# First products of the token and channel mixing in two steps, and one DVE stretch for a head's output

## The chip, the cores and the metric

The kernel runs as one program on one core of a Trainium2 chip. The metric is the device time of one execution in microseconds (us). Five engines work side by side: TensorE (PE, with its weight loads shown apart as PEld), VectorE (DVE), ScalarE (ACT), GpSimd (POOL), and SyncE (SP), whose queue issues the DMA transfers. Each engine takes its own instructions in program order and waits for others by semaphores.

## What is computed

The reference chains three blocks, for a batch of 4, 8 heads, 576 positions and 64 numbers per head. Everything is float32 at the ends.

```
scores = q k^T / sqrt(D) + (cum_i - cum_j), causal        # cum = running sum of log f
attn   = exp(scores - max);  attn /= sum(attn) + 1e-9
x      = attn v                                            # [4, 576, 512]
h      = relu(x^T w_tok1) w_tok2                           # token mixing, over the positions
u      = x + h^T
y      = u + relu(u w_ch1) w_ch2                           # channel mixing, 512 -> 1536 -> 512
out    = (g * sigmoid(g)) w_out,  g = conv3(relu(y w_in))  # gated block, 512 -> 1024 -> 512
```

## The kernel before

**Splitting.** Products of the mixing blocks are made in float16 with each operand as a pair, a high part h and a low part l = value - h. One product of two pairs takes three matmuls, wh·xh, wh·xl and wl·xh. The helper `mm3` (lines 277 to 282) issues them in this order, and lines 280, 281 and 282 in the profile are these three, whoever called it.

**Loops.** There are 32 heads (batch times 8). Scores are made for pairs of heads (`score`), then `smax` (DVE) takes the row maximum, `sexp` (ACT) the exponential, and the result is transposed: by PE for the first 8 heads and the last (`ptr`), by a DMA for the others, which first splits it on POOL and DVE (`hi_part`, `lo_part`; the lines 1027 and 1033, tiles `ph` and `pl`). `pv` multiplies it with the values and, in a 65th column, sums it. `norm` (DVE) makes the reciprocal of the sum, and `xout` (DVE) writes the scaled x of the head, tile `xf`. `x_hi` (ACT) and `x_lo` (POOL) split it into `xh` and `xl`.

Four heads are a group (8 groups, two to a batch). For a group `t1` multiplies with w_tok1 (two calls with `a` = 0, 1; each 5 terms, 15 matmuls of 128x256), and `t2` with w_tok2, four times, onto a transpose of x. `u_copy` takes u to SBUF. Once both groups of a batch are there, `u_largest` (DVE, line 266, tile `um`), `u_span` (PE, line 260) and `u_scale` (DVE, tile `su`) find a power of two for the batch, and `u_part` splits u into `uh` (ACT) and `ul` (DVE, line 594), two halves of 288 positions, of which each comes in two steps.

`channel_mix` works on such a half: `m1` multiplies with a block of w_ch1 (per block four calls, `k` = 0 to 3, each three matmuls of 128x288), `rh` and `rl` apply the ReLU and split, `m2` multiplies with w_ch2. Of 12 blocks, 5 are done while the attention runs; the rest and the gated block come after it.

**What sets the order.** Every step is written down as a task with its engine, an estimated duration, a rank, the keys it reads and writes, and the PSUM ring it takes (`z`: 2 double banks, `w`: 4 banks). The planner `Order.run` simulates the engines with these estimates, takes at each point the open task that can begin first (ties by rank), and the instructions are written in that order. So a change to a task, a key or a rank moves instructions everywhere in the first half of the program. The constants that set the ranks are `TOKR`, `TOKP`, `VRANK`, `SETR`, `LATER` and `PER`.

In a task of `t1` all of `xh` and `xl` of the four heads are read; every task of `m1` reads all eight parts of u (`ukeys`: four of `uh`, four of `ul`).

## Time and profile before

| | us |
|---|---|
| median of 3 executions | 717.89 (717.03 to 718.03) |
| span of the profiled execution | 718.1 |
| PE busy | 698.7 (97% of the span), 6417 matmuls |
| PE weight loads | 561.1 (78%) |
| DVE busy | 507.4 (71%) |
| ACT busy | 428.5 (60%) |
| POOL busy | 243.4 (34%) |
| chain that ended last: on PE, on DVE | 87%, 8% |

The profiled execution is known by its span, which is within 0.1 us of the slowest of the three that were timed. The span can be read in two halves. Up to about 315 us attention, token mixing and the early channel mixing run interleaved; from there to the end PE works through the late channel mixing and the gated block. [...]

### The profile page before, as it was taken

How to read it: one execution, taken by the hardware profiler on the slowest of the kernel's cores; microseconds unless marked ns; L12 is line 12 of the kernel's file. 1: busy time of each engine (PE TensorE's matmuls, PEld its weight loads, DVE VectorE, ACT ScalarE, POOL GpSimd, SP SyncE). 2: the span in 40 equal slices, each digit the busy share in tenths (PEclk: the TensorE clock that was granted, in tenths of full speed). 3: DMA queues.
4: the chain of work that ended last, by engine and by line, in shares of the span. 5: the costliest groups of instructions: out<-in, count | busy, mean ns of one | idle time of the engine just before them, and what ended most of it. 6: DMA issues, size and time to landing. Idle time of an engine off the chain costs nothing.

```text
span 718.1 us, 16399 instructions
## 1 busy us (share of the span) xinstructions
PE 698.7 (97%) x6417; PEld 561.1 (78%) x6417; DVE 507.4 (71%) x1268; ACT 428.5 (60%) x940; POOL 243.4 (34%) x321
## 2 busy tenths in 40 slices
PE   6999888999999999999999999999999999999998
PEld 5889665878877788888888778778888778778786
DVE  6787878999987779537566857435778866875570
ACT  6987776586666544646574645112177766776671
POOL 2247562748453666240000212103023322322240
PEclk9999887999999999999999999999999999999999
DMA  9445769799995979785455765344211111100101
GB/s 225 141 127 189 193 175 235 120 258 226 248 239 138 199 122 223 189 282 150 144 172 147 250 221 161 99 133 144 66 56 58 51 59 34 51 27 25 34 17 50
DMA packets 153117, 101.98 MB, mean 142 GB/s; under 512 B 90000, under 2 KB 145168, under 8 KB 153040
## 3 DMA queue, kind: packets, MB, share of 16 engines
q1 hardware_dynamic: 152944, 100.79, 54.4%
q8 instruction: 50, 0.82, 0.5%
q14 instruction: 27, 0.22, 0.1%
q10 hardware_dynamic: 96, 0.15, 0.1%
HBM read 57.73 MB, written 23.59 MB: 113 GB/s over the span
## 4 chain that ended last, share of the span: by engine, by line
PE 87%; DVE 8%; ACT 1%; DMA 1%; SPq 1%; issue 1%; POOL 0%; DVEq 0%; ACTq 0%
PE w L280 15%; PE w L281 15%; PE w L282 15%; PE z L281 8%; PE z L282 8%; PE z L280 8%; PE z L994 6%; PE w L1083 3%; DVE pl L1033 2%; PE w L1051 2%; PE w L1235 2%; PE z L998 1%; PE w L260 1%; DVE ul L594 1%; PE w L1088 1%; PE w L1089 1%
## 5 line engine op out<-in xcount | busy, mean ns | idle before, releaser
L282 PEld LDWEIGHTS <-w 128*128 128x128 f16 x1280 | 125.6, 98 | 34.0 <-issue 1.9
L280 PEld LDWEIGHTS <-w 128*128 128x128 f16 x1280 | 125.3, 98 | 33.7 <-issue 2.4
L281 PEld LDWEIGHTS <-w 128*128 128x128 f16 x1280 | 125.3, 98 | 33.0 <-issue 1.7
L281 PE MATMUL w<-ul,w 128*128 128x288 f16 x416 | 120.0, 288 | 1.6 <-DVE ul L594 1.6
L280 PE MATMUL w<-uh,w 128*128 128x288 f16 x416 | 120.0, 289 | 1.3 <-ACT uh L591 1.1
L282 PE MATMUL w<-uh,w 128*128 128x288 f16 x416 | 119.9, 288 | 0.0
L275 POOL TENSOR_TENSOR g<-sg,g 128x286 f16<-128x286 f32 (+1 forms) x64 | 55.1, 867 | 150.8 <-ACT g L269 148.0
L1518 DVE SCALAR_TENSOR_TENSOR cv<-hp,cw,cv 128x286 f32<-128x286 f32 (+1 forms) x128 | 75.0, 593 | 38.3 <-ACT cv L1512 36.0
L1018 ACT ACTIVATE t<-t,m 128x192 f32<-128x192 f32 (+4 forms) x160 | 82.0, 551 | 18.1 <-DVE m L1012 14.9
L643 ACT ACTIVATE r<-w 128x288 f16<-128x288 f32 x96 | 39.3, 409 | 88.0 <-PE w L282 87.1
L1012 DVE CUSTOM_DVE_ANT_0 t<-z,mask 128x192 f32<-128x192 f32 (+4 forms) x160 | 70.3, 479 | 12.8 <-PE z L998 12.5
L720 POOL TENSOR_TENSOR p<-p,u 128x288 f32<-128x288 f32 x32 | 26.6, 863 | 149.7 <-DMA p<-p_d 115.1
L647 DVE SCALAR_TENSOR_TENSOR r<-w,r 128x288 f16<-128x288 f32 x96 | 43.3, 453 | 46.8 <-ACT r L643 46.2
L281 PE MATMUL z<-g,w 128*128 128x286 f16 (+1 forms) x256 | 73.3, 286 | 0.0
L280 PE MATMUL z<-g,w 128*128 128x286 f16 (+1 forms) x256 | 73.0, 285 | 0.0
L282 PE MATMUL z<-g,w 128*128 128x286 f16 (+1 forms) x256 | 72.9, 285 | 0.0
L280 PE MATMUL w<-vh,w 128*128 128x288 f16 x224 | 64.1, 286 | 0.0
L281 PE MATMUL w<-vl,w 128*128 128x288 f16 x224 | 64.1, 286 | 0.0
L282 PE MATMUL w<-vh,w 128*128 128x288 f16 x224 | 64.1, 286 | 0.0
L280 PE MATMUL z<-r,w 128*128 128x288 f16 x224 | 64.1, 286 | 0.0
L281 PE MATMUL z<-r,w 128*128 128x288 f16 x224 | 64.1, 286 | 0.0
L282 PE MATMUL z<-r,w 128*128 128x288 f16 x224 | 64.1, 286 | 0.0
(201 smaller groups left out, 1686.8 us busy)
## 6 DMA issues: line engine op xcount, KB each, us to landing
wraw<-in_moe_w_ch_dram SPq DMA_DIRECT2D x24, 512.0 KB, 4.2
qk<-in_qk_dram SPq DMA_DIRECT2D x15, 608.0 KB, 5.4
u_d<-us SPq DMA_DIRECT2D x8, 576.0 KB, 3.4
p_d<-res SPq DMA_DIRECT2D x32, 144.0 KB, 3.1
p<-p_d SPq DMA_DIRECT2D x8, 576.0 KB, 5.3
u<-u_d SPq DMA_DIRECT2D x8, 576.0 KB, 4.8
x_d<-p SPq DMA_DIRECT2D x8, 576.0 KB, 3.2
u<-x_d SPq DMA_DIRECT2D x8, 576.0 KB, 3.9
```

What stands on the lines that cost most here:

```text
L275: nc.gpsimd.tensor_tensor(o, a, b, ALU.subtract)
L280: nc.tensor.matmul(ps, wh, xh, start=(first and i == 0), stop=False)
L281: nc.tensor.matmul(ps, wh, xl, start=False, stop=False)
L282: nc.tensor.matmul(ps, wl, xh, start=False, stop=(last and i == n - 1))
L643: nc.scalar.activation(out=t[:, 0, :], in_=box["z", m], func=AF.Relu)
L647: nc.vector.scalar_tensor_tensor(t[:, 1, :], box["z", m], 0.0, f32(t[:, 0, :]), ALU.max, ALU.subtract)
L720: nc.gpsimd.tensor_tensor(box["p"][:, d], box["p"][:, d], box["u"][:, d], ALU.add)
L994: nc.tensor.matmul(out_[x], t[r, Q0[i]:Q0[i] + 128], t[r, k0:k0 + n], start=first, stop=False)
L1012: nc.vector.tensor_tensor_reduce(to, z_t.pop((n, i)), mk, -0.125, 3e38, ALU.add, ALU.min, m_t[n][0:rows, i:i + 1])
L1018: nc.scalar.activation(out=tt[0:rows, o:o + w], in_=tt[0:rows, o:o + w], func=AF.Exp, bias=m_t[n][0:rows, i:i + 1], scale=-1.0)
L1083: nc.tensor.matmul(o[:, 0:65], p32(n)[:, 128 * blk:128 * blk + 128], vp32_t[g % 2][:, slot, hh, :], start=(j == 0), stop=(j == nb - 1))
L1518: nc.vector.scalar_tensor_tensor(cv, hp_t[m][:, s0 + t:s1 + t], cw[:, t, m:m + 1], cv, ALU.mult, ALU.add)
```

## The change

`mm3` stays for the second products. For `t1` and `m1` two helpers take its place. `mm_high` issues the two matmuls with a high x (wh·xh, wl·xh), `mm_low` the one with a low x (wh·xl). `t1` becomes two tasks for each `a`: 10 matmuls that read `xh` only, then 5 that read `xl`. `m1` becomes five tasks for each block: four of 2 matmuls, `k` = 0 to 3, that each read only their own part of `uh`, and a fifth (`k` = 4) of 4 matmuls that reads all of `ul`. The number of matmuls is the same.

`norm` and `xout` become one task of three DVE instructions. The keys of `opening` are widened: the first writer of a half of u now claims all its parts.

The constants of the ranks change, and with them the order of the whole first half. The planner's durations are split with the tasks (`t1` 1.66 into 1.11 and 0.55, `m1` into MM * 2 and MM * KD).

```diff
-    TOKR, TOKP = 4.0, 5.0
-    VRANK = 10.0
-    SETR = ((-15.0, 20.0),)
-    LATER = (-60.0, 0.0, 20.0)
-    PER = 7.0
+    TOKR, TOKP = 4.32, 4.98
+    VRANK = 19.68
+    SETR = ((-10.9, 9.83),)
+    LATER = (-62.89, 79.29, 41.56)
+    PER = 7.03
...
+    def mm_high(ps, terms, first=True):
+        for i, (wh, wl, xh) in enumerate(terms):
+            nc.tensor.matmul(ps, wh, xh, start=(first and i == 0), stop=False)
+            nc.tensor.matmul(ps, wl, xh, start=False, stop=False)
+
+    def mm_low(ps, terms, last=True):
+        for i, (wh, xl) in enumerate(terms):
+            nc.tensor.matmul(ps, wh, xl, start=False, stop=(last and i == len(terms) - 1))
...
-        return {"reads": [("first", r - 1)], "writes": [("first", r)]}
+        return {"reads": [("first", r - 1)], "writes": [("first", r)] + [x for k in range(KD) for x in split_keys(r, k)]}
...
             wh, wl = halves("ch1", m)
+            if k == KD:
+                mm_low(box["z", m], [(wh[:, x, :], ul[:, x, :]) for x in range(KD)])
+                return
             if k == 0:
                 box["z", m] = flat_bank(tag)[:, 0:CH]
-            mm3(box["z", m], [(wh[:, k, :], wl[:, k, :], uh[:, k, :], ul[:, k, :])], k == 0, k == KD - 1)
+            mm_high(box["z", m], [(wh[:, k, :], wl[:, k, :], uh[:, k, :])], k == 0)
...
             for j in range(KD):
-                T("PE", MM * 3, rank + pe, m1, m, j, reads=[*ukeys, wkey("ch1", m)],
+                T("PE", MM * 2, rank + pe, m1, m, j, reads=[uhigh[j], wkey("ch1", m)],
                   writes=[kz, kr, (*kr, "l")], ring=[kz])
+            T("PE", MM * KD, rank + pe, m1, m, KD, reads=ulow, writes=[kz], ring=[kz])
...
             nc.vector.reciprocal(rs, rs)
-            rs_t[n] = rs
-
-        def xout(n):
             g, hh = divmod(n, HG)
...
-            o, rs = pv_t.pop(n), rs_t.pop(n)
+            o = pv_t.pop(n)
             nc.vector.tensor_tensor(x_of(n), o[:, :, 0:64], rs.unsqueeze(2).to_broadcast([128, NS, D]), ALU.mult)
...
-                T("DVE", 0.5, rank + 6, norm, n, reads=[kw, ("vsc", g % 3)], writes=[("rs", n % 2)], pools=A1, ring=[kw])
-                T("DVE", 0.46, rank + 6, xout, n, reads=[kw, ("rs", n % 2)], writes=[("xf", g % 2, n % HG)], pools=A1, ring=[kw])
+                T("DVE", 0.98, rank + 6, norm, n, reads=[kw, ("vsc", g % 3)], writes=[("xf", g % 2, n % HG)], pools=A1, ring=[kw])
...
-        def t1(g, a):
+        def t1(g, a, low):
             st = tok[g]
+            c = slice(a * 128, (a + 1) * 128)
+            if low:
+                mm_low(st["ps1", a], [(w1h[:, j, c], st["xl"][:, j, :]) for j in range(NS)])
+                return
             st["ps1", a] = bank("w")[:, 0:HG * D]
-            c = slice(a * 128, (a + 1) * 128)
-            terms = []
-            for j in range(NS):
-                terms.append((w1h[:, j, c], w1l[:, j, c], st["xh"][:, j, :], st["xl"][:, j, :]))
-            mm3(st["ps1", a], terms)
+            mm_high(st["ps1", a], [(w1h[:, j, c], w1l[:, j, c], st["xh"][:, j, :]) for j in range(NS)])
...
-                T("PE", 1.66, t0 + 3, t1, g, a, reads=[*xk, *W1K], pools=A1, ring=[kw],
+                T("PE", 1.11, t0 + 3, t1, g, a, False, reads=[*xk["xh"], *W1K], pools=A1, ring=[kw],
                   writes=[kw, ("t1h", a), ("t1l", a)])
+                T("PE", 0.55, t0 + 3, t1, g, a, True, reads=xk["xl"], pools=A1, ring=[kw], writes=[kw])
```

Three places show what the new order does.

The first is on DVE, at the last head of group 1 (head 7), whose x the group's `t1` needs. `um<-us` is `u_largest` of group 0, `rs` and `xf` are the sum's reciprocal and x of head 7, `pl` the low split of heads 8 (t_194) and 9 (t_195). Before:

```order
L266 TENSOR_REDUCE um_87<-us 128x1
L555 SCALAR_TENSOR_TENSOR w_123<-w_113,pw_c_238,w_123 128x512
L1033 SCALAR_TENSOR_TENSOR pl<-t_194,ph 128x640
L1095 TENSOR_SCALAR rs<-w,vsc 128x5
L1098 RECIPROCAL rs<-rs 128x5
L1033 SCALAR_TENSOR_TENSOR pl<-t_195,ph 128x1024
L1106 TENSOR_TENSOR xf<-w,rs 128x5x64
```

Now:

```order
L1045 SCALAR_TENSOR_TENSOR pl<-t_195,ph 128x1024
L1045 SCALAR_TENSOR_TENSOR pl<-t_195,ph 128x640
L266 TENSOR_REDUCE um_87<-us 128x1
L330 TENSOR_SCALAR wraw<-wraw 128x512
L331 SCALAR_TENSOR_TENSOR w_118<-w_118,wraw 128x512
L1107 TENSOR_SCALAR rs<-w,vsc 128x5
L1110 RECIPROCAL rs<-rs 128x5
L1115 TENSOR_TENSOR xf<-w,rs 128x5x64
```

All low splits of heads 8 and 9 now stand ahead of the group's reduction, the three instructions of head 7 stand together, and a weight decode (`wraw`, `w_118`) stands ahead of them. On PE, the first sums of `pv` of head 8 now stand directly ahead of `t1` of group 1, and the pair of scores that stood between `pv` of head 7 and `t1` now stands ahead of `t2` of group 0.

The second is on DVE, at the scale of batch 0 (`su`), on which `uh` and `ul` rest. Before:

```order
L266 TENSOR_REDUCE um_87<-us 128x1
L1097 TENSOR_SCALAR rs<-w 128x5
L1098 RECIPROCAL rs<-rs 128x5
L1033 SCALAR_TENSOR_TENSOR pl<-t_196,ph 128x1024
L237 TENSOR_REDUCE su_73<-w 128x1
L238 TENSOR_SCALAR su_73<-su_73 128x1
L240 TENSOR_SCALAR su_73<-su_73 128x1
L241 TENSOR_SCALAR su_73<-su_73 128x1
L242 TENSOR_SCALAR su_73<-su_73 128x1
L1106 TENSOR_TENSOR xf<-w,rs 128x5x64
L1033 SCALAR_TENSOR_TENSOR pl<-t_196,ph 128x640
L594 SCALAR_TENSOR_TENSOR ul<-us,su_73,uh 128x576
```

Now:

```order
L266 TENSOR_REDUCE um_87<-us 128x1
L1109 TENSOR_SCALAR rs<-w 128x5
L1110 RECIPROCAL rs<-rs 128x5
L1115 TENSOR_TENSOR xf<-w,rs 128x5x64
L237 TENSOR_REDUCE su_73<-w 128x1
L238 TENSOR_SCALAR su_73<-su_73 128x1
L240 TENSOR_SCALAR su_73<-su_73 128x1
L241 TENSOR_SCALAR su_73<-su_73 128x1
L242 TENSOR_SCALAR su_73<-su_73 128x1
L330 TENSOR_SCALAR wraw<-wraw 128x512
L331 SCALAR_TENSOR_TENSOR w_120<-w_120,wraw 128x512
L603 SCALAR_TENSOR_TENSOR ul<-us,su_73,uh 128x576 x3
```

The split `pl` of 1024 columns has left the place ahead of the scale, x of head 9 has come there, and between the scale and the first `ul` a weight decode stands where x and a `pl` of 640 columns stood.

The third is on PE, at the start of `t1` of group 2 (`w1h`). Before, a pair of scores (lines 994 and 998) and, ahead of it, `m1` (`uh`):

```order
L282 LDWEIGHTS w_115
L282 MATMUL w<-uh,w_115 128x288
L994 MATMUL z<-qk_149 128x288 x4
L998 MATMUL z<-dec,sel 128x288 x4
L280 LDWEIGHTS w1h
L280 MATMUL w<-xh,w1h 128x256
L281 LDWEIGHTS w1h
L281 MATMUL w<-xl,w1h 128x256
```

Now:

```order
L1101 LDWEIGHTS pt
L1101 MATMUL w<-vp_206,pt 128x64
L1102 LDWEIGHTS pt
L1102 MATMUL w<-vp_206,pt 128x65
L286 LDWEIGHTS w1h
L286 MATMUL w<-xh,w1h 128x256
L287 LDWEIGHTS w1l
L287 MATMUL w<-xh,w1l 128x256
```

`t1` of group 2 now follows directly on the last `pv` of head 11, which is the group's last head; the pair of scores comes behind it.

## Rows read from the trace of the kernel before

**Rows 1.** The page's slices: PE's busy share and granted clock, in tenths.

```profile
PE   6999888999999999999999999999999999999998
...
PEclk9999887999999999999999999999999999999999
```

**Rows 2.** Busy time by stretch: engine busy (instructions), clock, DMA share, GB/s.

```profile
80.00:100.00 20.00, 17.15 (x150) 13.31 (x151) 15.56 (x33) 13.63 (x25) 11.13 (x15) 0.83 0.70 168
100.00:120.00 20.00, 14.58 (x124) 9.46 (x120) 18.14 (x46) 13.49 (x28) 8.32 (x9) 0.83 1.04 232
87.00:92.80 5.80, 5.80 (x28) 4.12 (x28) 3.98 (x9) 3.02 (x4) 4.36 (x6) 0.50 0.51 95
87.00:103.00 16.00, 16.00 (x172) 12.36 (x172) 11.42 (x31) 10.88 (x22) 9.74 (x11) 0.82 0.58 153
136.30:139.60 3.30, 3.30 (x31) 2.83 (x30) 3.30 (x4) 1.11 (x2) 3.30 (x3) 1.00 0.05 10
```

**Rows 3.** Timeline of PE at t1 of group 1: start, us, instruction [idle before].

```profile
83.31 0.49 PE L260 MATMUL w<-ident,vacc 128*128 128x128 f32 x2
85.38 0.27 PE L280 MATMUL w<-xh,w1h 128*128 128x256 f16 x1 [1.58 <-ACT xh L269]
86.91 0.37 PE L281 MATMUL w<-xl,w1h 128*128 128x256 f16 x1 [1.27 <-POOL xl L275]
```

**Rows 4.** Timeline of DVE, ACT and POOL there, the way of head 7's x.

```profile
83.23 1.19 DVE L1033 SCALAR_TENSOR_TENSOR pl<-t,ph 128x1024 f16<-128x1024 f32 x1
84.34 0.48 DVE L1106 TENSOR_TENSOR xf<-w,rs 128x320 f32<-128x320 f32 x1
84.86 0.47 ACT L269 ACTIVATE xh<-xf 128x320 f16<-128x320 f32 x1 [0.92 <-DVE xf L1106]
85.41 1.45 POOL L275 TENSOR_TENSOR xl<-xf,xh 128x320 f16<-128x320 f32 x1 [1.51 <-ACT xh L269]
```

**Rows 5.** DMA issues: operation, count, median us to landing.

```profile
pt<-pl SPq DMA_TRANSPOSE x23, 4.8
```

**Rows 6.** Timeline of DVE: a weight decode, and head 8's three instructions together.

```profile
95.75 0.41 DVE L321 TENSOR_SCALAR wraw<-wraw 128x512 int32<-128x512 int32 x1
96.20 0.70 DVE L322 SCALAR_TENSOR_TENSOR w<-w,wraw 128x512 int32<-128x512 int32 x1
98.22 0.17 DVE L1097 TENSOR_SCALAR rs<-w 128x5 f32<-128x5 f32 x1 [1.32 <-PE w L1090]
...
98.64 0.49 DVE L1106 TENSOR_TENSOR xf<-w,rs 128x320 f32<-128x320 f32 x1
```

**Rows 7.** Timeline of DVE at the scale of batch 0.

```profile
102.47 1.35 DVE L266 TENSOR_REDUCE um<-us 128x1 f32<-128x1152 f32 x1 [0.29 <-ACT us L1251]
...
104.04 1.31 DVE L1033 SCALAR_TENSOR_TENSOR pl<-t,ph 128x1024 f16<-128x1024 f32 x1
105.27 0.41 DVE L237 TENSOR_REDUCE su<-w 128x1 f32<-128x256 f32 x1
...
107.48 1.34 DVE L594 SCALAR_TENSOR_TENSOR ul<-us,su,uh 128x576 f16<-128x576 f32 x1
```

**Rows 8.** Timeline of PE there: the first products of the channel mixing.

```profile
106.92 0.40 PE L280 MATMUL w<-uh,w 128*128 128x288 f16 x1 [1.10 <-ACT uh L591]
108.88 0.40 PE L281 MATMUL w<-ul,w 128*128 128x288 f16 x1 [1.56 <-DVE ul L594]
```

**Rows 9.** Timeline of DVE: head 11's first instruction, and what stood idle ahead of it.

```profile
116.04 0.46 DVE L647 SCALAR_TENSOR_TENSOR r<-w,r 128x288 f16<-128x288 f32 x1 [1.33 <-ACT r L643]
...
124.53 0.17 DVE L1097 TENSOR_SCALAR rs<-w 128x5 f32<-128x5 f32 x1 [1.04 <-PE w L1090]
...
131.47 0.15 DVE L1097 TENSOR_SCALAR rs<-w 128x5 f32<-128x5 f32 x1
```

**Rows 10.** Timeline of PE at t1 of group 2.

```profile
134.92 1.24 PE L994 MATMUL z<-qk 64*128 64x288 f32 x8
...
136.36 0.28 PE L280 MATMUL w<-xh,w1h 128*128 128x256 f16 x1
```

More of the change, by code (lines that the diff above doesn't have):

```diff
@@ L619, in chunk @@
             rd = [ku, ("scale", id(scale))]
-            T("ACT", 0.77, rank + evac, piece, k, 0, reads=[*rd, *o["reads"]], writes=kh + o.get("writes", []))
+            T("ACT", 0.77, rank + evac, piece, k, 0, reads=[*rd, *o["reads"]], writes=o.get("writes", kh))
             T("DVE", 0.78, rank + evac, piece, k, 1, reads=[*rd, *kh], writes=kl)
@@ L628, in channel_mix @@
         back, back_key = backs[:, part, b:b + 1], ("back", part, b)
-        r, ukeys = u_of
+        r, uhigh, ulow = u_of
         box = {}
@@ L729, in mix_input @@
             T("POOL", 0.86, rank, add_u, d, reads=[ku], writes=[(kp, d)])
-        return (r, kv), (box, kp)
+        return (r, [kv[0]] * KD, [kv[1]]), (box, kp)
     def mix_output(c, p_of, rank):
@@ L963, in fox_moe_kernel @@
         pv_t = {}
-        rs_t = {}
         SETS = {(4,): DEC4, (0, 3): 0, (1, 2): DEC12}
@@ L1285, in group @@
             b, half = divmod(g, GB)
-            xk = [(x, k) for x in ("xh", "xl") for k in range(HG)]
+            xk = {x: [(x, k) for k in range(HG)] for x in ("xh", "xl")}
             xf = [("xf", g % 2, k) for k in range(HG)]
@@ L1315, in group @@
                 chunks[0] += 1
-                early_u[2 * b + e] = r, [x for k in range(KD) for x in split_keys(r, k)]
+                early_u[2 * b + e] = r, *([split_keys(r, k)[y] for k in range(KD)] for y in range(2))
                 for h in range(GB):
@@ L1322, in group @@
                     T("ACT", 0.77, t0 + 4, u_part, gg, e, 0, reads=[*uk, ("scale", id(su[b])), *o["reads"]],
-                      writes=kh + o.get("writes", []), pools=A1)
+                      writes=o.get("writes", kh), pools=A1)
                     T("DVE", 0.78, t0 + 4, u_part, gg, e, 1, reads=[*uk, ("scale", id(su[b])), *kh], writes=kl, pools=A1)
```

## The prediction

> **What bounds the kernel now.** I read the page's slices first. PE is busy in nine tenths or more of nearly every slice; it falls short in the first, and in slices 5 to 7, where the granted clock falls with it [rows 1]. [...] The stretches of 20 us then say where that is: from 80 to 120 us PE is busy for 17.15 and 14.58 of 20 us, so it stands idle for 8.3 us there, and the mean clock is 0.83 [rows 2]. From 87.0 to 103.0 us it stands full, with 16.00 of 16.00 [rows 2]. So the losses lie in a few gaps around it, and the timelines of PE show them with the engine that ended each.
>
> Gap A, `t1` of group 1: PE waits 1.58 us for `xh`, makes one product, waits 1.27 us for `xl`, and only then runs [rows 3]. The run that follows is slow: 28 matmuls in 5.80 us at clock 0.50, 0.207 us each, where the same products of group 2 take 3.30 us for 31 at 1.00, 0.106 us each [rows 2]. Behind the gap stands DVE: between the reciprocal and x of head 7 it makes a `pl` of 1.11 us (83.23 to 84.34), then ACT needs 0.47 for `xh` and POOL 1.45 for `xl` [rows 4].
>
> Gap B, the scale of batch 0: from `um` at 102.47 DVE takes until 105.27 to begin the scale, with a `pl` of 1.23 us in between (104.04 to 105.27) [rows 7]. PE makes one product at 106.92, after 1.10 us of waiting for `uh`, and the second at 108.88, after 1.56 us for `ul` [rows 8].
>
> From gap B on DVE sets the pace as much as PE does. From the scale at 105.27 to head 11's reciprocal at 131.47 [rows 7, 9] lie 26.2 us, in which the two longest idle stretches of DVE are 1.33 and 1.04 us [rows 9].
>
> **The change part by part.**
>
> *Gap A.* Two things of this gap go. `xl` (1.27) no longer holds the products: 10 matmuls read `xh` alone, at 0.106 us about 1.06 us of work [rows 2], and `xl` takes 1.45 after `xh` [rows 4], so at most 0.4 us of it is left over. And the `pl` of 1.11 us no longer stands between reciprocal and x. The three instructions together take 0.91 us (98.22 to the end of x at 99.13) [rows 6], and `xh` another 0.5. The scores that covered PE there have moved ahead; what is left between head 7's `pv` and `t1` is two spans of 0.49 us [rows 3] and the first sums of head 8. So PE waits about 1.41 - 0.98, some 0.4 us, where it waited 2.85: 2.45 us gained. The bounds are 1.3 (only the wait for `xl` goes) and 2.85. If the gap is that small, I take it that the clock doesn't fall, since it fell in this gap and stays at 1.00 where PE runs full [rows 1, 2]: 30 matmuls by 0.101 us, 3.0 us. Together 5.5. What follows up to 103 us is full on PE [rows 2], so the lead is carried there.
>
> *Gap B.* The `pl` of 1.23 us goes from ahead of the scale, and x of head 9 comes in: 0.91 us after the 1.27 of the reduction, so the scale begins 2.2 us after `um` instead of 2.8: 0.6 us earlier. The first 16 products then need only the first two `uh`, and run for 16 by 0.121, 1.9 us (the spacing is that of 0.106 at 288 instead of 256 columns, an estimate). `ul` comes later than before: the decode ahead of it takes 1.15 [rows 6], and two `ul` have to be made, 1.27 (107.48 to 108.75) and about 0.8. So the low step waits about 0.7 us. When it begins, PE is 14 products further than it was then, 1.7 us, less a span of 0.49 that now comes later. At the scale itself the lead is 5.5 + 0.6, about 6.1 us.
>
> *From there to `t1` of group 2.* DVE's list between the scale and head 11 is longer now: one decode (1.15 [rows 6]) and three `rl` (about 0.4 each [rows 9]) come in, 2.35 us. A weight split comes in too, and x of head 9, a `pl` of 640 columns and two small maxima go out; that exchange I estimate, by their widths against the rows of the same kind, at 0.95 us less. It leaves 1.4 us more. If DVE's idle 2.4 us [rows 9] vanish, it takes 1.0 us less than before; if they stay, 1.4 more. So the lead at head 11 is 4.7 to 7.1, in the middle 5.9. Lower clock or waits on PE in this stretch cost nothing more, as long as DVE is the later one.
>
> *A new wait.* `t1` of group 2 now stands directly behind head 11's `pv`, and PE's next work stands behind it. From that reciprocal it takes 0.91 and 0.5 us to `xh`. With a lead of 5.9 `t1` begins at 131.47 - 5.9 + 1.41, at 127.0; before, it began at 136.36 behind scores that took 1.44 (134.92 to 136.36) [rows 10], which now follow. The lead is then 134.92 - 127.0, about 7.9. But PE has run ahead of DVE by then and stands idle ahead of `t1`, for some 3.5 us by my count of the products in between. I take it that the clock falls there as it did in gap A, whose wait was shorter: 30 products by 0.101, 3.0 us. The lead left is 4.9; with the bounds of head 11, 3.7 to 6.1, and 7.9 or more if the clock stays up.
>
> *The rest.* The start (PE's first slice) keeps its order up to the first transposes; I count it at nothing, as what fills PE there waits for loads that haven't moved. From 140 us on PE is at nine tenths in every slice [rows 1]. The moved constants shuffle the order there, which can open or close waits of a microsecond. I take 0, with 2 us either way. On SP's queue the second transpose of head 10 now stands behind three stores of `uh` and `ul`, which wait for ACT and DVE; ahead of its `pv` PE has eight blocks of `m1`, over 10 us, so I count it at nothing, and at most at the 4.8 of a transpose [rows 5] if that cover is gone. On POOL the low part of a token weight has moved behind one `ph`; the scores and sums of a head lie between it and `t2`, its reader. The products of the second half stay the same on a full PE, so a lead that comes so far comes to the end.
>
> The sum: 718.1 - 4.9, about **713.2**. It is made against the profiled span of 718.1, which is 0.2 above the median of 717.89; I don't correct for that.
>
> **The rivals.**
>
> *More comes back.* The clock stays up ahead of `t1` of group 2 too, because the first half-clock stretch sits behind a longer standstill than mine: 718.1 - 7.9 gives 710.2, and with 2 us of the later waits 708. For it: the gap may be filled by products that I count as done. Against it: DVE is the later one there.
>
> *DVE takes the gain.* The gain at A is there, but `um`, the scale and the decode in front of `ul` come as DVE gets to them: the lead falls to the 2.45 of gap A's wait, and a clock that falls at B and at group 2 takes 3.0 of what the first one gave. 718.1 - 2.45 + 1.4 (DVE's longer list) gives 717. For it: DVE stands full from gap B on. Against it: the idle stretches in rows 9 end with PE and ACT, not with DVE.
>
> *Slower: the first sums of head 8.* They stand ahead of `t1` of group 1 now, and behind them PE can do nothing else. They need the transposes of head 8, of which the last is issued after `pl` of 640 columns and lands 4.8 us later (the median of 23) [rows 5]. I count that `pl` early enough by about 1 us. If it comes 3 us later than that, PE stands 2 us longer than in gap A's old order, the clock falls as before (nothing of the 5.5 is gained), and group 2's new wait costs its 3.0 at the lower clock: 718.1 + 2 + 3.0 - 1.2 (gap B's products) gives 722. It decides from about 1 us of lateness, where the gain at A begins to go, and turns the sign at about 3.5.
>
> [...]
>
> **How the numbers follow.** Forecast (4.9 earlier, 710.5 to 716) 0.50; more comes back (707 to 710.5) 0.17; DVE takes the gain (716 to 718.5) 0.18; slower (above 718.5) 0.15. The range that holds 8 in 10 runs from 708.0 to 719.0. A measurement of this kernel tells about 0.2% from no change, 1.4 us: faster means below 716.5, slower above 719.3. Of the case in which DVE takes the gain I give a third to the faster side. Faster 0.73, same 0.14, slower 0.13.
>
> **What would show it.** In the profile after, `t1` of group 1 should begin about 2 us earlier and run at 0.106 us a product; the granted clock of the slices from 80 to 100 us should be near 1.00. The first products of the channel mixing should run on `uh` without the 1.56 us for `ul`, about 6 us earlier. A wait for `xh` of some 3 us should stand ahead of `t1` of group 2. It is wrong if PE waits for `pt` ahead of `t1` of group 1, if the clock falls again behind gap A, or if the waits that go reappear between 130 and 300 us.

## The result, and the profile after the change

The changed kernel takes 725.05 us (median of 4, 722.70 to 725.59) against 717.48 (717.03 to 718.03): a ratio of 1.0102, with an interval of 1.0083 to 1.0121. It is slower by 1%, where 713.2 had been forecast. The profiled execution has a span of 720.7 us; it is the fastest of the four (722.70 us).

The kernel before was profiled a second time (the run before_again): span 714.2, time 715.97. The span of 718.1 that the prediction was made from is 3.9 us longer than this one. The profiles held against each other from here on are those of 714.2 and 720.7, 6.5 us apart. Both executions lie below the median of their kernel, by 1.5 and 2.35 us, and the medians are 7.6 us apart. First the page's slices of the changed kernel (PE's busy share, and its granted clock in tenths of full speed), as in [rows 1].

```profile
PE   7999889789999999999999999999999999999998
...
PEclk9999999999999999999999999999999999999999
```

The dip that stood in slices 5 to 7 is shallower there, and a new one follows: slice 8 (126 to 144 us) has 7 tenths. The busy times by stretch, as in [rows 2] (PE, weight loads, DVE, ACT, POOL; granted clock), show it in us: first before_again,

```profile
80.00:100.00 20.00, 17.15 (x163) 13.33 (x163) 17.79 (x42) 14.04 (x28) 12.30 (x17) 0.91 0.68 175
100.00:120.00 20.00, 14.40 (x154) 9.80 (x151) 18.72 (x50) 14.37 (x28) 6.82 (x7) 0.91 1.13 257
120.00:140.00 20.00, 19.36 (x238) 15.91 (x235) 18.06 (x49) 12.65 (x28) 16.19 (x14) 1.00 0.75 144
140.00:160.00 20.00, 19.71 (x212) 15.19 (x211) 17.80 (x56) 16.51 (x36) 7.98 (x10) 1.00 1.04 241
```

then the changed kernel:

```profile
80.00:100.00 20.00, 17.30 (x170) 14.55 (x168) 17.83 (x47) 14.28 (x27) 15.45 (x20) 0.91 0.97 229
100.00:120.00 20.00, 16.96 (x169) 13.37 (x168) 18.99 (x43) 15.52 (x33) 5.44 (x7) 1.00 0.90 221
120.00:140.00 20.00, 15.35 (x182) 11.95 (x181) 18.24 (x48) 12.19 (x24) 14.10 (x14) 0.91 0.65 142
140.00:160.00 20.00, 17.25 (x201) 13.09 (x200) 18.84 (x49) 15.18 (x32) 9.93 (x10) 0.98 1.07 242
```

From 80 to 100 us PE is about as busy as in before_again. From 100 to 120 it gains 2.6 us. From 120 to 160 it loses 6.5 (19.36 + 19.71 - 15.35 - 17.25). That this is also the distance of the spans is chance, since the gain has to be taken off. Over the whole span PE stands idle for 23.9 us (720.7 - 696.8 busy) where before_again has 18.7 (714.2 - 695.5), and it is busy 1.3 us longer with the same number of matmuls. About a quarter of the 5.2 us of added idle time lies outside the stretches from 80 to 160 us; its two largest waits are 1.30 us for `m` at 47.85 and 0.86 us for `xh` at 250.21. The waits behind the stretches are five lines of PE's timeline in the changed kernel (start, us, instruction, and in brackets the idle time ahead of it with what ended it); the first answers [rows 3], the next two [rows 8], the fourth [rows 10].

```profile
88.27 0.37 PE L286 MATMUL w<-xh,w1h 128*128 128x256 f16 x1 [2.70 <-ACT xh L269]
106.07 0.28 PE L286 MATMUL w<-uh,w 128*128 128x288 f16 x1 [1.85 <-ACT uh L600]
108.61 0.65 PE L291 MATMUL w<-ul,w 128*128 128x288 f16 x4 [0.17 <-DVE ul L603]
131.88 0.30 PE L286 MATMUL w<-xh,w1h 128*128 128x256 f16 x1 [4.65 <-ACT xh L269]
158.94 2.00 PE L1006 MATMUL z<-qk 64*128 64x64 f32 x8 [2.75 <-DVE m L1024]
```

The split does its work: behind 106.07 sixteen products run on `uh`, and `ul` costs 0.17 us where it cost 1.56 [rows 8]. But `t1` of group 1 still waits 2.70 us, `t1` of group 2 waits 4.65, and a score waits 2.75 us for the maxima that free its bank. Before_again reached `t1` of group 2 like this, without a wait (PE's timeline again):

```profile
131.70 1.24 PE L994 MATMUL z<-qk 64*128 64x288 f32 x8
...
133.13 0.28 PE L280 MATMUL w<-xh,w1h 128*128 128x256 f16 x1
```

In the changed kernel these scores come behind `t1`. Its 131.88 is therefore to be held against 131.70: all that PE had won by then is gone.

### The profile page after: what moved, and what is told of

It is laid out like the page before. It is cut to its first block, busy times and chain, and to the rows that moved or that the text cites. A ratio compares the mean times of both kernels' runs of the same rounds, so it can differ in the third digit from the quotient of the medians.

```text
span 720.7 us, 16401 instructions
## 1 busy us (share of the span) xinstructions
PE 696.8 (97%) x6417; PEld 561.6 (78%) x6417; DVE 514.6 (71%) x1268; ACT 427.3 (59%) x940; POOL 244.5 (34%) x321
## 4 chain that ended last, share of the span: by engine, by line
PE 89%; DVE 5%; POOL 2%; issue 2%; ACT 1%; SPq 1%; DMA 0%; DVEq 0%; POOLq 0%; ACTq 0%
PE z L281 8%; PE z L280 8%; PE z L282 8%; PE w L286 8%; PE w L287 8%; PE w L291 8%; PE w L280 8%; PE w L282 8%; PE w L281 8%; PE z L1006 6%; PE w L1095 3%; PE z L1010 1%; PE w L1063 1%; PE w L1100 1%; PE w L1101 1%
## 5 line engine op out<-in xcount | busy, mean ns | idle before, releaser
L280 PEld LDWEIGHTS <-w 128*128 128x128 f16 x896 | 87.4, 98 | 23.2 <-issue 1.4
L282 PEld LDWEIGHTS <-w 128*128 128x128 f16 x896 | 87.7, 98 | 22.2
L281 PEld LDWEIGHTS <-w 128*128 128x128 f16 x896 | 87.4, 98 | 22.4 <-issue 0.6
L282 PE MATMUL w<-uh,w 128*128 128x288 f16 x256 | 73.2, 286 | 0.0
L281 PE MATMUL w<-ul,w 128*128 128x288 f16 x256 | 73.2, 286 | 0.0
L280 PE MATMUL w<-uh,w 128*128 128x288 f16 x256 | 73.2, 286 | 0.0
L1006 PE MATMUL z<-qk 64*128 64x288 f32 (+4 forms) x384 | 60.5, 426 | 4.1 <-DVE m L1024 4.1
L275 POOL TENSOR_TENSOR xl<-xf,xh 128x320 f16<-128x320 f32 x32 | 29.7, 929 | 87.8 <-ACT xh L269 87.8
L1039 POOL TENSOR_SCALAR ph<-t 128x1024 f16<-128x1024 f32 (+1 forms) x46 | 49.4, 1087 | 25.2 <-ACT t L1030 22.5
```

Source lines behind the costliest of these rows:

```text
L275: nc.gpsimd.tensor_tensor(o, a, b, ALU.subtract)
L280: nc.tensor.matmul(ps, wh, xh, start=(first and i == 0), stop=False)
L281: nc.tensor.matmul(ps, wh, xl, start=False, stop=False)
L282: nc.tensor.matmul(ps, wl, xh, start=False, stop=(last and i == n - 1))
L1006: nc.tensor.matmul(out_[x], t[r, Q0[i]:Q0[i] + 128], t[r, k0:k0 + n], start=first, stop=False)
L1039: nc.gpsimd.tensor_scalar(h_t[n][:, sl], t_t[n % TB][:, sl], PSC, 0.0, ALU.mult, ALU.add)
```

## The experiments

All ratios are those to the kernel before on the same chip. Each expectation names its theories by letters (there is no C); they changed as results came in.

### Is it the order or the parts?

**new_code_old_numbers**: the changed kernel, its constants set back.

```diff
-    TOKR, TOKP = 4.32, 4.98
+    TOKR, TOKP = 4.0, 5.0
...
-    PER = 7.03
+    PER = 7.0
```

> The changed kernel, with the five lines of due times set back to their values of before (TOKR, TOKP, VRANK, SETR, LATER, PER). Theory A, the order is at fault (the new numbers place so much work on DVE ahead of heads 7 and 11 that PE runs dry in front of t1 of groups 1 and 2, while the split products help): 710 to 717 us, clearly under the changed kernel's 725. Theory B, the split itself or the joined norm is at fault (both uh and ul of a chunk claimed with the first part, one more step per block, three DVE instructions in a row): 722 to 727 us, like the changed kernel.

Measured: 725.59 us, 1.0112 (1.0094 to 1.0130).

**old_code_new_numbers**: the kernel before with the new constants (the same lines, the other way).

> The kernel before with the changed kernel's due times (TOKR, TOKP, VRANK, SETR, LATER, PER) and nothing else. Theory A (order at fault): 722 to 730 us, slower than before by as much as the changed kernel or more, since nothing splits the products to save time. Theory B (split or norm at fault): 715 to 719 us, no loss.

Measured: 730.25 us, 1.0195 (1.0154 to 1.0236). So the constants are not the cure: set back in the changed kernel they bring nothing (725.59 against 725.05), and put alone into the kernel before they cost 2%. Theory A as it was first written (the new numbers are at fault, while the split products help) falls with the run above it.

**m1_only**, **t1_only** and **norm_only**: one part each in the kernel before, with the old constants, placed by the planner. The parts of the diff:

```diff
# m1_only
-                T("PE", MM * 3, rank + pe, m1, m, j, reads=[*ukeys, wkey("ch1", m)],
+                T("PE", MM * 2, rank + pe, m1, m, j, reads=[uhigh[j], wkey("ch1", m)],
...
+            T("PE", MM * KD, rank + pe, m1, m, KD, reads=ulow, writes=[kz], ring=[kz])
# t1_only
-                T("PE", 1.66, t0 + 3, t1, g, a, reads=[*xk, *W1K], pools=A1, ring=[kw],
+                T("PE", 1.11, t0 + 3, t1, g, a, False, reads=[*xk["xh"], *W1K], pools=A1, ring=[kw],
...
+                T("PE", 0.55, t0 + 3, t1, g, a, True, reads=xk["xl"], pools=A1, ring=[kw], writes=[kw])
# norm_only
-                T("DVE", 0.5, rank + 6, norm, n, reads=[kw, ("vsc", g % 3)], writes=[("rs", n % 2)], pools=A1, ring=[kw])
...
+                T("DVE", 0.98, rank + 6, norm, n, reads=[kw, ("vsc", g % 3)], writes=[("xf", g % 2, n % HG)], pools=A1, ring=[kw])
```

> The kernel before with one part of the change: the channel mixing's first products take uh first and ul in a step of their own, with the keys of a chunk claimed as in the change; token mixing, norm and due times as before. By the trace the wait of 1.56 us for ul goes and the 16 products of a block run while ul is still made, worth 2 to 5 us at that place if nothing comes back: 712 to 716 us for Theory A. Theory B with the claimed keys as the cause: 719 to 724 us.

Measured: 723.81 us, 1.0092 (1.0070 to 1.0114).

> The kernel before with one part of the change, as the planner places it with the old numbers: t1 as a high and a low step. Issued at the old places this was worth 0.1% (715.8 against 717.1). Theory A: 720 to 727 us. Theory B' with m1 alone at fault: 715 to 718 us.

Measured: 718.42 us, 1.0022 (1.0012 to 1.0032): slower, but by less than the 720 expected.

> The kernel before with one part of the change, as the planner places it with the old numbers: a head's sum, reciprocal and x as one task of 0.98 us. Issued at the old places this part was worth nothing that can be measured (716.3 against 717.1). Theory A (any re-planned order loses against one whose numbers were fitted to its tasks): 720 to 727 us. Theory B' (only the split of m1 and of t1 disturbs the order): 715 to 718 us.

Measured: 735.55 us, 1.0259 (1.0246 to 1.0273), the slowest of all, by the part that only joins two tasks. Its profile has 9.3 us of waits for `m` ahead of scores, where before_again has 1.6, and PE is busy for 707.0 us in it, where before_again has 695.5 with the same number of matmuls.

Every one of the six re-planned orders is slower than before, by 0.2 to 2.6%, and they don't add up: the three parts alone cost 1, 6 and 18 us, together (new_code_old_numbers) 8. Nor do they lose at one place. In new_code_old_numbers PE waits for `xh` ahead of `t1` of group 2, as in the changed kernel; m1_only has no wait there, and its longest is one for `m` at a score:

```profile
131.52 0.27 PE L286 MATMUL w<-xh,w1h 128*128 128x256 f16 x1 [3.44 <-ACT xh L269]
...
118.77 2.25 PE L1007 MATMUL z<-qk 64*128 64x64 f32 x8 [3.34 <-DVE m L1025]
```

**frozen_all**, **frozen_m1**, **frozen_t1**, **frozen_norm**: the parts without the planner. It sees the old tasks, so that all else stays in the order of before; only what is issued at their places differs.

```diff
# m1
-            mm3(box["z", m], [(wh[:, k, :], wl[:, k, :], uh[:, k, :], ul[:, k, :])], k == 0, k == KD - 1)
+            mm_high(box["z", m], [(wh[:, k, :], wl[:, k, :], uh[:, k, :])], k == 0)
+            if k == KD - 1:
+                mm_low(box["z", m], [(wh[:, x, :], ul[:, x, :]) for x in range(KD)])
# t1
-            mm3(st["ps1", a], terms)
+            mm_high(st["ps1", a], [x[:3] for x in terms])
+            mm_low(st["ps1", a], [(x[0], x[3]) for x in terms])
# norm
             rs_t[n] = rs
+            joined_x(n)
```

> All three parts of the change, but in the order of the kernel before: the planner still sees the old tasks, and only what is issued at their places differs (a block of m1 issues its eight high products and then its four low ones, t1 likewise, and a head's x is issued right behind its reciprocal). After the runs so far (old code with new numbers 730, new code with old numbers 726, one part alone 724) Theory A reads: any re-planned order loses 6 to 13 us, the parts themselves gain. It expects 713 to 716 us here: the waits of 1.3 us for xl and 1.6 us for ul go, and some of it comes back. Theory B (the parts cost by themselves): 719 us or more. Theory D (PE's gain before 120 us is given back, since VectorE sets the pace until head 11): 716 to 718 us, no difference, with a new wait of 2 to 4 us ahead of t1 of group 2.

> The order of before; only the first products of channel mixing are issued high first, low last within each block. Theory A: 715 to 716.5 us (1.6 us of wait for ul go). Theory B: 719 or more. Theory D: 717 to 718, the wait moves to t1 of group 2.

> The order of before; only t1 is issued high first, low last. Theory A: 715.5 to 717 us (1.3 us of wait for xl go at t1 of group 1). Theory B: 719 or more. Theory D: 717 to 718, PE waits the longer for what comes next.

> The order of before; only a head's x is issued right behind its sum and reciprocal, ahead of the one to four VectorE tasks that stood between them for 23 of the 32 heads. For head 7 the decode of the next head (1.1 us) stood between, and PE waited 1.6 us for xh: Theory A: 715.5 to 717 us (xh 1.1 us earlier, the decode 0.5 us later). Theory B with the joined norm as the cause: 719 or more. Theory D: 717 to 718.

Measured: frozen_all 716.50 us, 0.9992 (0.9984 to 1.0001); frozen_m1 717.03, 0.9994 (0.9982 to 1.0005); frozen_t1 715.78, 0.9987 (0.9978 to 0.9995); frozen_norm 716.30, 0.9991 (0.9980 to 1.0003). Issued at the old places the parts cost nothing that can be measured; Theory B is out. Nor do they bring much: the medians differ by at most 0.2%, and the lowest end of the four intervals is 0.9978. Between Theories A and D these runs don't decide: frozen_t1 and frozen_norm lie in A's ranges, frozen_all and frozen_m1 in D's. The waits on PE in frozen_all show where the gain goes (engine, line and what was waited for: total, times, longest):

```profile
PE w L260 <- DVE um L266: 2.0, 1, 2.0
PE w L260 <- ACT junk L890: 1.7, 2, 1.4
...
PE w L286 <- ACT uh L600: 1.5, 1, 1.5
...
PE w L286 <- ACT xh L269: 0.6, 1, 0.6
```

At `t1` of group 1 the waits for `xh` and `xl` fall from 2.85 us [rows 3] to 0.6, as the parts were meant to do. Then PE waits 2.0 us for `um`, for which before_again waits 0.3. In its two stretches from 80 to 120 us PE is busy for 18.25 and 13.48 us, before_again for 17.15 and 14.40: what is won in the first is given back in the second. That is Theory D's mechanism, but not at its place: it had put the new wait ahead of `t1` of group 2, where frozen_all has none. Of these four only frozen_t1 has its whole interval below 1.

### Is it how much VectorE has to do?

**after_light** and **before_light**: both kernels with the decode of a weight block cut to one instruction. They leave out the lowest three bits of the weights.

```diff
-        nc.vector.tensor_scalar(low, low, 29, None, ALU.logical_shift_right)
-        nc.vector.scalar_tensor_tensor(c, c, 3, low, ALU.logical_shift_left, ALU.bitwise_or)
+        nc.vector.tensor_scalar(c, c, 3, None, ALU.logical_shift_left)
```

> The changed kernel with less work on VectorE in the first 165 us: the decode of a weight block is one instruction (0.4 us) instead of two (0.42 and 0.69), which leaves out the weights' lowest three bits. 25 blocks by 0.69 are some 17 us of VectorE less; the order is untouched. Theory D (VectorE's amount of work sets the pace between 80 and 160 us): 713 to 717 us, and within 2 us of the kernel before with the same cut. Theory E (single places in its list): 718 to 722 us, still 4 us or more over the kernel before with the same cut.

> The kernel before with the same cut in the decode (the weights' lowest three bits are left out, 17 us less of VectorE). Theory D: 712 to 716 us. Theory E: 713 to 717 us; what tells the two apart is the distance to the changed kernel with the cut.

Measured: after_light 720.65 us, 1.0041 (1.0027 to 1.0056); before_light 715.12, 0.9969 (0.9957 to 0.9980). DVE's busy time falls by 32 us in the changed kernel and by 29 in the kernel before over the whole program; by the expectation's count half of it (25 of 50 blocks) lies in the first part. That brings 2.4 us to the kernel before and 4.4 to the changed one; 5.5 us stay between them, so VectorE's amount of work carries about 2 of the 7.6, and the two runs fall as Theory E had it (4 us or more between them). In after_light's timeline of PE the wait ahead of `t1` of group 2 is still there, 4.66 us against 4.65:

```profile
132.91 0.37 PE L286 MATMUL w<-xh,w1h 128*128 128x256 f16 x1 [4.66 <-ACT xh L269]
```

### Can single moves mend it?

Here the planned order was kept and a few tasks were put elsewhere in an engine's list. The moves are given in words.

**norms_early**: two moves in the changed kernel.

```diff
+    MOVES = [("DVE", norm(7), ahead of u_largest(0)),
+             ("DVE", norm(11), ahead of smax(12, 2))]
```

> The changed kernel with two moves on VectorE's list and nothing else: head 7's sum, reciprocal and x go ahead of the maximum u_largest(0) and a weight decode, head 11's go ahead of smax(12,2), smax(12,1), lo_part(12,0) and one low(). In the changed kernel's trace pv(7) was done at 84.5 us and its sum began at 86.75; pv(11) was done at 127.2 and its sum began at 130.4, while PE waited 2.7 and 4.65 us for the xh of these heads. Theory E (the places in VectorE's list cost the time): t1 of group 1 comes 2 us earlier, t1 of group 2 waits 1 to 2 us instead of 4.65, and the time falls from 725 to 717 to 721. Theory D (VectorE has too much to do there, whatever the order): what was passed becomes late, the waits for m and pt grow by as much, 723 to 726.

Measured: 725.95 us, 1.0121 (1.0102 to 1.0140). No gain: PE waits 3.62 us ahead of `t1` of group 1, put down to a statistic of v on DVE (`vsc`), and 5.27 us for `xh` ahead of `t1` of group 2. The sums came early, the casts didn't. Three lines of ACT's timeline in this run; the last is the cast of head 11, whose input was there at 131.8:

```profile
88.61 0.66 ACT L571 ACTIVATE wraw<-w 128x512 f32<-128x512 f32 x1 [4.27 <-DVE w L376]
...
134.76 0.72 ACT L605 ACTIVATE w<-w,pw_c 128x512 f16<-128x512 f32 x1 [1.07 <-DVE w L609]
135.39 0.45 ACT L314 ACTIVATE xh<-xf 128x320 f16<-128x320 f32 x1
```

ACT waits 4.27 and 1.07 us for the very DVE instructions that had been passed (the decode, a weight's low part), and `xh` stands behind them on its list.

**norms_casts_early**: the casts moved as well.

```diff
+    MOVES = [("DVE", norm(7), ahead of u_largest(0)), ("DVE", u_largest(0), ahead of smax(11, 4)),
+             ("DVE", the decode, ahead of smax(11, 4)), ("ACT", x_hi(7), ahead of the squares),
+             ("DVE", norm(11), ahead of smax(12, 2)), ("ACT", x_hi(11), ahead of sexp(12, 2))]
```

> The changed kernel with the heads' sums early as in norms_early, and now their casts too. In that run the sum of head 7 was done at 86.1 us and that of head 11 at 131.7, but ScalarE made xh only at 89.25 and 135.4: its list held a weight's squares (waiting for the decode that had been passed) and a weight's scaling (waiting for a low() that had been passed) ahead of them. Here x_hi(7) goes ahead of those squares, x_hi(11) ahead of sexp(12,2) on ScalarE, and u_largest(0) and the decode go behind v_pow(3) on VectorE, since t1 of group 1 then waited for the bank that v_pow(3) frees. Theory E (single places in the lists cost the time): t1 of group 1 starts at 86 to 87 us (88.3 in the changed kernel), t1 of group 2 at 127 to 129 (131.9) with a wait under 2.5, and the time is 717 to 721. Theory D (the engines are so matched there that any gain is paid elsewhere): the waits for m at the scores and for pt grow by what t1 gains, 723 to 726.

Measured: 726.85 us, 1.0140 (1.0127 to 1.0153). `t1` of group 1 now waits 0.61 us and starts at 86.7, as expected; and then PE's timeline shows these waits:

```profile
105.79 0.80 PE L309 MATMUL w<-ident,um 128*128 128x128 f32 x2 [3.80 <-DVE um L315]
...
132.60 0.27 PE L335 MATMUL w<-xh,w1h 128*128 128x256 f16 x1 [1.71 <-ACT xh L318]
...
138.97 0.78 PE L340 MATMUL w<-xl,w1h 128*128 128x256 f16 x4 [4.02 <-POOL xl L324]
```

What group 1 gains comes back at `um` (3.80 us, where the changed kernel waits 1.01), and the 2.9 us of group 2 at `xl` on POOL. Theory E (mending single places) fell in both runs. Theory D had the time right in the first and 0.85 us too low in the second, and the second pays at `um` and `xl`, not at the scores and `pt` it had named.

**frozen_plus** and **frozen_plus2**: the same attempt in the order of before, at the scale of batch 0, where frozen_all waits.

```diff
# frozen_plus, on top of frozen_all
+    MOVES = [("DVE", u_largest(1), ahead of smax(10, 0)), ("DVE", u_scale(0), ahead of smax(10, 1)),
+             ("DVE", two u_part low, ahead of lo_part(10, 0)), ("ACT", u_copy(1, 1, 1), ahead of x_hi(8)),
+             ("ACT", two u_part high, ahead of v_squares(4)), ("PE", v_span(4), ahead of score(6, [4]))]
# frozen_plus2
-             ("ACT", two u_part high, ahead of v_squares(4))
+             ("ACT", two u_part high, ahead of sexp(10, 1))
```

> The three parts in the order of before (716.5 us), and eight moves around the scale of batch 0, where PE waited 2.0 us for um, 1.4 for a statistic of v and 1.5 for uh: the last copy of u goes ahead of a head's cast on ScalarE, um goes ahead of four smax on VectorE, the scale ahead of smax(10,1), two ul ahead of lo_part(10,0), two uh ahead of the squares of v on ScalarE, and v's span behind the first block of m1 and more on PE. By the times in that trace uh is ready at 103.9 us instead of 106.65: 2.7 us less wait. Theory E: 712.5 to 715 us. Theory D: the gain comes back as a wait for heads 10 and 11 ahead of t1 of group 2: 716 to 718 us.

> The three parts in the order of before with the moves of frozen_plus, and the two uh now ahead of sexp(10,1) on ScalarE. In that run the scale was done at 101.98 us, but uh began at 103.5, behind two exponentials that waited for m; PE waited 3.45 us for it. Theory E: uh begins at 101.9, PE starts the first channel product at 102.8 instead of 104.3, 713.5 to 715.5 us. Theory D: the 1.5 us come back as waits for m ahead of the scores of heads 12 and 13 or ahead of t1 of group 2, 716 to 717.

Measured: frozen_plus 716.20 us, 0.9985 (0.9974 to 0.9996), within a microsecond of frozen_all; frozen_plus2 718.85, 1.0024 (1.0015 to 1.0033). In the second, PE begins the channel products at 102.7 us instead of 106.65, but then waits 0.93 and 0.87 us for `ul` and 0.89 and 1.15 for `m` (frozen_all: 0.93 and 0.64 for `m`), and its granted clock from 100 to 120 us is 0.66, against 0.79 in frozen_all. Theory E fell in both runs; frozen_plus lies in Theory D's range, frozen_plus2 above both. Beside frozen_t1, frozen_plus is the only kernel that computes the same and has its whole interval below 1, by 0.1 to 0.2%; nothing here that computes the same beats the kernel before by more.

### Which part of the planned order holds the loss?

**old_then_new** and **new_then_old**: the changed code with an order joined from two. The lists of all engines follow one order up to the span of `um` of batch 0, about 104 us, and the other from there. The orders are given in words.

```diff
-        order = sorted(range(n), key=lambda k: (begun[k], k))
+        order = first 483 tasks in the order of before, the rest in the planned order    # old_then_new
+        order = first 478 tasks in the planned order, the rest in the order of before    # new_then_old
```

> The changed code, with its three parts, in the order of before up to the span of um of batch 0 (the first 483 of 3448 tasks, about 104 us), and in the planned order of the changed kernel for all that is left. Theory F (the planned order loses in its first 104 us: VectorE comes 4.6 us later to head 7 than in before_again): 715 to 718 us. Theory G (it loses behind the scale of batch 0, where the channel products are used up ahead of pv(10) and nothing is left to run ahead of t1 of group 2): 721 to 726 us, with a wait of 3 to 5 us for xh ahead of t1 of group 2 and 2.7 us for m at a score near 159 us.

> The other half: the changed code in its planned order up to the span of um of batch 0 (the first 478 tasks), and in the order of before for the rest. Theory F: 721 to 726 us. Theory G: 715 to 718 us, with no wait over 1 us between 120 and 165 us.

Measured: old_then_new 724.01 us, 1.0102 (1.0087 to 1.0116), the changed kernel's own ratio; new_then_old 718.25, 1.0023 (1.0008 to 1.0039). Theory G holds, and the waits agree; new_then_old is a quarter of a microsecond above G's range, so a small loss, some 0.2%, stays with the first part or with the joint. PE's timeline in old_then_new has the two of the changed kernel again:

```profile
134.63 0.37 PE L332 MATMUL w<-xh,w1h 128*128 128x256 f16 x1 [4.65 <-ACT xh L315]
...
161.85 1.31 PE L1052 MATMUL z<-qk 64*128 64x64 f32 x8 [2.75 <-DVE m L1070]
```

In new_then_old the 2.70 us ahead of `t1` of group 1 stay,

```profile
89.02 0.37 PE L332 MATMUL w<-xh,w1h 128*128 128x256 f16 x1 [2.70 <-ACT xh L315]
```

but from 120 us on PE is nearly full (busy times by stretch, columns as above):

```profile
120.00:140.00 20.00, 19.37 (x226) 15.48 (x227) 19.17 (x55) 14.04 (x29) 13.36 (x14) 1.00 0.80 171
140.00:160.00 20.00, 19.19 (x223) 15.09 (x221) 19.37 (x45) 13.52 (x30) 9.77 (x10) 1.00 0.88 221
```

The joints have waits of their own. At about 106 us old_then_new waits 3.51 us for `uh`, where the changed kernel waits 1.85 and frozen_all 1.53, and new_then_old waits 3.98 us at 109.98 for a statistic of v:

```profile
106.72 0.40 PE L332 MATMUL w<-uh,w 128*128 128x288 f16 x1 [3.51 <-ACT uh L646]
...
109.98 0.80 PE L306 MATMUL w<-ident,vacc 128*128 128x128 f32 x2 [3.98 <-ACT junk L938]
```

So some 2 us of old_then_new's 7.6 may be the joint's. What is left, 5 to 6 us, is still three times the 1.8 us that new_then_old loses with its joint.

Most of the loss lies behind the scale of batch 0. In the order of before, ten tasks of `m1` (30 products) and a pair of scores stand between the last `pv` of head 11 and `t1` of group 2; in the planned order of the changed kernel nothing does, since these blocks of `m1` are done ahead of that `pv`. DVE needs its time for head 11 either way, and DVE's timeline in the changed kernel shows what stands on its list between the end of that `pv` (131.88 - 4.65, 127.2 us) and head 11's first instruction:

```profile
127.48 0.47 DVE L1024 CUSTOM_DVE_ANT_0 t<-z,mask 128x320 f32<-128x320 f32 x1
...
128.17 1.22 DVE L1045 SCALAR_TENSOR_TENSOR pl<-t,ph 128x1024 f16<-128x1024 f32 x1
129.30 1.20 DVE L564 SCALAR_TENSOR_TENSOR w<-w,pw_c,w 128x512 f16<-128x512 f32 x1
130.43 0.15 DVE L1109 TENSOR_SCALAR rs<-w 128x5 f32<-128x5 f32 x1
...
133.98 0.34 DVE L1024 CUSTOM_DVE_ANT_0 t<-z,mask 128x192 f32<-128x192 f32 x1
```

In before_again head 11's first instruction comes at 128.15, 0.1 us after its `pv`, against 3.2 us here, and PE has its `m1` until `xh` is made. The last line is the last of the maxima that free the two banks of `z`. The pair of scores that before_again runs ahead of `t1` takes both banks, so with DVE's list as it is it could not have filled the gap here, whatever its place on PE.

That the order behind 104 us carries most of the loss is shown by the two joined runs. That it is the used-up `m1` is read from the two orders and the trace, and was not tried alone: `m1` put back behind `pv` without the rest of the old order was not run. Nor does it hold for every re-planned order: m1_only loses 6 us without this wait. Not settled either is why norm_only lost as much as 18 us.

**before_again**, the second profile of the unchanged kernel, is used throughout.

> The unchanged kernel, profiled a second time, for a second look at how its profiled execution stands to its median of 717.5. If the first profile of before (span 718.1) was an ordinary execution, this one again has a span near 718 and the idle times of rows 3 and 8. If it was a slow one, the span here is 715 to 716 and the difference of some 2.5 us is to be found in the granted clock between 80 and 120 us or at the end.

Measured: 715.97 us, span 714.2. The difference lies in the clock, as the second case had it; it is larger than it said (3.9 us of span) and reaches a little later: see the last section.

## Why the prediction was wrong, point by point

Two steps failed above all. The lead of 5.5 us that gap A was to give did not come: 0.13 us of it is left at `um` of batch 0. And the order behind the scale, put at 0, lost most of what was lost: with the order of before from there on the same code stands at 1.0023, with the planned order at 1.0102.

**The base of the sum.** The forecast was counted from 718.1 as if span and time were one, and the table of before put that execution within 0.1 us of the slowest of the three timed. In the runs on record the kernel before takes 1.7 to 1.9 us more than its span, so that execution took about 720, some 2.5 above the median of 717.48. As a base 718.1 is only 0.6 us off that median; the harm is that the clock was read from a slower execution than the median one. The waits at `t1` of group 1, 1.58 and 1.27 us, are the same in before_again.

**Gap A.** The step "PE waits about 1.41 - 0.98, some 0.4 us" failed: 2.70. It reckoned from the end of PE's `pv`, as if DVE were waiting there, although the order printed with the change shows `um` and a decode ahead of head 7. The `pv` of head 7 on PE, and DVE's timeline in the changed kernel, which answers to [rows 4]:

```profile
81.15 3.46 PE L1095 MATMUL w<-vp,pt 128*128 128x65 f32 x30
...
81.65 2.46 DVE L1045 SCALAR_TENSOR_TENSOR pl<-t,ph 128x1024 f16<-128x1024 f32 x2 [0.62 <-POOL ph L1039]
84.03 1.34 DVE L266 TENSOR_REDUCE um<-us 128x1 f32<-128x1152 f32 x1
85.29 0.81 DVE L330 TENSOR_SCALAR wraw<-wraw 128x512 int32<-128x512 int32 x1
86.14 0.69 DVE L331 SCALAR_TENSOR_TENSOR w<-w,wraw 128x512 int32<-128x512 int32 x1
86.75 0.22 DVE L1107 TENSOR_SCALAR rs<-w,vsc 128x5 f32<-128x5 f32 x1
```

The `pv` of head 7 was done at 84.6 us; DVE came to its sum at 86.75. The 3.0 us for the clock failed with it: the clock falls here again, to 0.91 from 80 to 100 us, as in before_again. In [rows 2] it had been 0.83, and that was one execution's price (last section). Of the lead of 5.5 us that was to be carried to 103 us, 0.13 arrived: `um` of batch 0 begins at 102.34 us (below), against 102.47 [rows 7].

**Gap B.** Right in mechanism. The scale begins 2.08 us after `um`, where it took 2.80 [rows 7] and 2.2 was forecast, 16 products run on `uh` alone, and PE waits 0.17 us for `ul` where 0.7 was forecast. DVE's timeline in the changed kernel:

```profile
102.34 1.34 DVE L266 TENSOR_REDUCE um<-us 128x1 f32<-128x1152 f32 x1
...
104.42 0.41 DVE L237 TENSOR_REDUCE su<-w 128x1 f32<-128x256 f32 x1
```

The lead was not there to add to: at the scale it is 0.85 us (105.27 to 104.42) where about 6.1 was forecast, and ahead of the first product PE waits 1.0 us for `um` and 1.85 for `uh`.

**From there to head 11.** "The lead at head 11 is 4.7 to 7.1": head 11's first instruction on DVE is at 130.43 us, against 131.47 in the profile of before [rows 9] and 128.15 in before_again. That is a lead of 1.0 us against the one and 2.3 us of lateness against the other.

**The new wait ahead of `t1` of group 2.** Right in place and about right in size: 4.65 us against 3.5, and some 1.7 at the lower clock against 3.0 (an estimate: the 20 products from 131.88 to 135.73 take 3.85 us, with a granted clock of 0.57 from 131.9 to 135.9, and 20 by the 0.106 of [rows 2] would take 2.1). Wrong was the lead it was set against: `t1` begins at 131.88 where 127.0 was forecast.

**The rest, "0, with 2 us either way".** Failed. The score at 158.94 costs 2.75 us, and the 8 us from 159 have a clock of 0.79. It is a place in the order that the prediction didn't look at, and the same wait, 2.67 to 2.75 us, comes in norms_early, norms_casts_early and old_then_new. The start was not free either: a score waits 1.30 us for `m` at 47.85, where before_again has no wait.

**The rivals.** DVE takes the gain (717) comes nearest for the parts: in the order of before they stay at 716.5, and the waits move to `um`. Its price for the new order was 1.4 us, DVE's longer list, where the re-planned orders cost 1 to 18. The slower rival had the right sign for another reason: the sums of head 8 came without waiting for their transposes, and what PE waited for at `t1` of group 1 was head 7. No rival said that the order behind the scale would lose by itself.

**The signs it named.** Two of its three signs of being wrong came: the clock fell again behind gap A, and waits reappeared behind 130 us. PE did not wait for `pt` ahead of `t1` of group 1. The wait for `xh` of some 3 us ahead of `t1` of group 2 came as forecast.

At two places PE kept the order of its list while it stood idle. In the changed kernel the pair of scores that before_again runs ahead of `t1` of group 2 stands behind it: PE waits 4.65 us for `xh`, and the scores begin at 136.91, behind the 30 products that began at 131.88. In gap A of before the first product of `w1l` with `xh`, which needs no `xl`, begins at 87.08, behind the one at 86.91 that waited 1.27 us for `xl` [rows 3].

## What to carry to other kernels

In this kernel the list schedule lost each time a task was split or joined or the numbers were changed: six re-planned orders cost 0.2 to 2.6%, while the same edits issued at the old places cost nothing. That the old numbers were fitted to the old tasks would explain it, and no run here shows it. So try an edit at frozen places first; it separates the edit from the reshuffle. When a change moves work, price the whole list ahead of each awaited instruction on the engine that makes it, not only the instruction, and ask what PE has left to do while it waits.

## What the runs showed of the hardware that was not expected

**Two executions of one kernel differ by 3.9 us, most of it in the clock.** PE is busy for 698.7 us in the one and 695.5 in the other, with the same matmuls, and the clock of the three stretches of 20 us from 80 to 140 is 0.83, 0.83 and 0.91 in the one, 0.91, 0.91 and 1.00 in the other. Two shorter stretches (columns as above), in the profile of before,

```profile
84.00:92.00 8.00, 5.36 (x26) 3.71 (x26) 6.86 (x17) 4.21 (x6) 5.12 (x6) 0.63 0.79 147
119.00:125.00 6.00, 5.36 (x65) 3.90 (x62) 4.54 (x25) 5.17 (x10) 1.87 (x2) 0.72 1.01 244
```

and before_again:

```profile
84.00:92.00 8.00, 6.08 (x58) 4.72 (x57) 6.61 (x18) 4.99 (x8) 5.76 (x7) 0.79 0.69 128
119.00:125.00 6.00, 5.36 (x77) 4.40 (x77) 5.14 (x20) 5.17 (x11) 3.93 (x4) 1.00 0.94 290
```

PE stands still for the same 2.85 us from 80 to 100 us in both, yet the clock is 0.63 in one and 0.79 in the other; and from 119 to 125 us, with PE busy for 5.36 us in both, 0.72 and 1.00 (before_again is 2 to 3 us ahead there, so the instructions are not the same). What a gap costs at the lower clock has to be taken from more than one profile.

**A decode on DVE took 2.35 us beside a POOL instruction.** In the changed kernel one decode on DVE takes 2.35 us, where it takes 0.70 in [rows 6] and the median of its line in this trace is 0.69; POOL subtracts a piece of `vp` at that time (timelines of DVE and POOL):

```profile
54.64 2.35 DVE L331 SCALAR_TENSOR_TENSOR w<-w,wraw 128x512 int32<-128x512 int32 x1
54.20 2.25 POOL L918 TENSOR_TENSOR vp<-vf,vp 128x1024 f16<-128x1024 f32 x1
```

They overlap for 1.8 us (54.64 to 56.45), and the decode is 1.65 longer. Not every DVE instruction beside one of POOL's is long. In the same trace a `pl` takes 0.81 us, the least of the 46 on its line, beside a POOL instruction that is on record all the while, and there it is POOL's that is long, 2.14 us where the fastest of its 32 take 0.53 and the median 0.54; a first `pl`, from 77.82, was running when it began:

```profile
79.47 0.81 DVE L1045 SCALAR_TENSOR_TENSOR pl<-t,ph 128x640 f16<-128x640 f32 x1
78.46 2.14 POOL L1137 TENSOR_SCALAR xf<-xf,tac 128x320 f32<-128x320 f32 x1
```

What makes the one long in the first pair and the other in the second, these traces don't show. DVE is busy for 514.6 us in the changed kernel and 506.6 in before_again, with the same number of instructions; but new_then_old has 515.2 and takes 718.25 us, so this sum by itself doesn't set the two kernels apart. Single instructions do differ, by 1.65 us here; that the order of the lists decides which ones is the author's guess, and no run tried it alone.
